# Two short conditionals and one copy of the further steps, in place of two branches that each hold a copy

## The chip, the cores and the metric

The kernel runs on one core of a Trainium2 chip. The metric is the device time of one execution in microseconds. The kernel before took 668.89 us, the median of three runs (668.12 to 669.98). A separate execution was taken by the hardware profiler, and every time inside the kernel below comes from that one: it took 649.77 us in all, of which 648.1 us lie between its first and its last instruction (the span).

The engines go by these names: PE is the matrix engine, PEld its loading of weights, DVE the vector engine, ACT the scalar engine, POOL the GpSimd engine, and SP the engine that here only issues DMA transfers. A "q" behind a name (PEldq, POOLq, SPq) is the sequencer of that engine, which reads instructions, branches, and waits for semaphores.

## What is computed

Attention within chunks of 64 tokens feeds a mixture of eight experts, in which each token goes to one expert only:

```python
batch, n_heads, seq, head_dim = (8, 8, 576, 64)
...
scores = scale * np.matmul(q_c, k_c.transpose(0, 1, 2, 4, 3))
...
attn = attn / (np.sum(attn, axis=-1, keepdims=True) + 1e-09)
out = np.matmul(attn, v_c)
...
N, D, E, F = (4608, 512, 8, 1024)
...
logits = xn @ en.T / tau
expert_idx = np.argmax(logits, axis=1)
...
for e in range(E):
    mask = expert_idx == e
    if not mask.any():
        continue
    h = np.maximum(x[mask] @ w1[e], 0.0)
    out[mask] = gate_w[mask, None] * (h @ w2[e])
```

The number of tokens of an expert is known only when the logits are. With the inputs of the reference the experts get 832, 359, 183, 448, 512, 1023, 576 and 675 tokens.

## The kernel before

**Attention and sorting.** Some 170 us of attention and routing come first. Each token's row is scattered by POOL into a table in device memory, `spots`, where the rows of one expert stand together, in groups of 64.

**Steps.** Then come the experts' steps. A step takes two groups at once: rows 0 to 63 of its block are a group that is counted from the low end of the experts, rows 64 to 127 one from the high end. The data fix how many steps are needed: with the counts above there are 73 groups (13, 6, 3, 7, 8, 16, 9 and 11); the first four steps are always two groups of the first and the last expert, and 65 groups are left. These make 32 pairs and one odd group. On the device the number of pairs is `n_steps` and the odd group is `n_odd`, 0 or 1; `groups` (L890) works them out on DVE, at 168.4 to 170.6 us.

Steps 0 to 35 are always run, by a loop that is unrolled (L1168). Step 36, `LEAST`, is the odd group, if there is one: it has 64 rows only. Steps 37 to 44 are run only if there are so many pairs; `more` (L1224) nests one conditional in the other for them, each on all five engines. With these inputs the odd group is there and none of the steps 37 to 44 is.

**One step.** SP loads its rows (`load_x`) and, where the expert changes, the weights (`load_w2` for the second layer, `load_late` for the first). The loads of weights are issued in every case and move nothing where their condition, read from a table, is 0. DVE turns the rows (`turn_xb`), ACT and DVE make the gate (`gates`), PE multiplies by the first layer (`hidden_plain`, or `hidden_fast` in the loop), ACT and DVE bring the result into shape, and `result` (L427) multiplies by the second layer on PE, scales by the gate on ACT (L447), and has POOL scatter the rows to `out` (L454). For the odd group the two halves of a row stand in the two halves of the block, so `result` has DVE compute the places of half rows first (L452).

**The end, which is what the change touches.** The order of every engine is written out by hand: an instruction stands where the program puts it, and waits on semaphores for others. The instructions of the odd group are laid around the result of step 35 (`before_last`), so that PE has something to do while ACT and DVE turn the odd group's hidden layer. Since that holds in one case only, there are two whole branches: with the odd group (hidden layer of 36, result of 35, result of 36, then `more` with all its eight nested steps), and without (result of 35, then `more` with all its eight nested steps again):

```python
with tc.If(odd_one > 0) as if_odd:
    step_alone(LEAST, before_last)
    more(LEAST + 1)
...
with if_odd.Else():
    ...
    before_last()
    ...
    more(LEAST + 1)
```

A conditional becomes a compare and branch on each engine (line L1228 for those of `more`, L1233 for the odd group). Where a body is not run, the engine jumps to a short block in which it raises its own semaphores by what the body would have added, and goes on from there; SP has nine such instructions, POOL waits for its scatters to have landed and raises its eight DMA semaphores with one instruction, INC_SWDGE_SEM. Line L1269 is the program's end: SP waits for every semaphore, POOL drains, and all five engines meet in two barriers.

Of the kernel before, what the change touches and what calls it, by code (L numbers as in the profile page):

```python
# [1 line left out]

# [16 lines left out]
P = 128  # L19
# [6 lines left out]
def kernel(  # L26
# [11 lines left out]
    nc = tc.nc  # L38
# [76 lines left out]

    n_steps = keep.tile([1, 1], I32, name="n_steps")
    n_odd = keep.tile([1, 1], I32, name="n_odd")
    second = keep.tile([P, 1], FP32, name="second")
    bp = ctx.enter_context(tc.tile_pool(name="blk", bufs=2))

    def whole(w):
# [87 lines left out]
    def gates(j):  # L209
        for _ in gate_parts(j):  # L210
            pass
# [212 lines left out]
        swap_next()  # L424
        turn(1)

    def result(j, ps_y):  # L427
        d = mo.pop(j)
        ps = ps_y.tile([P, D], FP32, tag="y", name="y_ps")
        one_group = j == LEAST  # L430
        w = D // 2 if one_group else D
        for c in range(KF):
            for r in range(P // Q):
                t0, s, d0 = (r % 2, 0, w * (r // 2)) if one_group else (r, r // 2, 0)
                nc.tensor.matmul(  # L435
                    ps[Q * r : Q * r + Q, 0:w],
                    lhsT=d["hT"][:, c, Q * t0 : Q * t0 + Q],
                    rhs=w2_sb[s][buf_of(j)][:, c, d0 : d0 + w],
                    start=(c == 0),
                    stop=(c == KF - 1),  # L440
                )
        if one_group:
            S = late_p.tile([P, 3, KD // 2, 2, Q], FP32, tag="S", name="S", bufs=2)
            y = S.rearrange("p a c b i -> p (a c b i)")
        else:
            y = bp.tile([P, D], FP32, tag="y", name="y", bufs=1)
        nc.scalar.activation(y[:, 0:w], ps[:, 0:w], AF.Copy, scale=gate_of.pop(j))  # L447
        to, at, bound = out, spot[:, j % SPOTS, TOK : TOK + 1].bitcast(I32), N - 1
        if one_group:

            at2 = bp.tile([P, 1], I32, tag="at2", name="at2")
            nc.vector.tensor_scalar(at2, at, 2.0, second, ALU.mult, ALU.add)  # L452
            to, at, bound = out.rearrange("n (s d) -> (n s) d", s=2), at2, 2 * N - 1
        ins = nc.gpsimd.indirect_dma_start(  # L454
            out=to,
            out_offset=bass.IndirectOffsetOnAxis(ap=at, axis=0),
            in_=y[:, 0:w],
            in_offset=None,
            bounds_check=bound,
            oob_is_err=False,  # L460
        )
        tc.declare_no_dep(ins.ins, group="rows", reason="blocks hold different tokens")
        tc.add_to_no_dep_group("rows", ins.ins)
# [8 lines left out]
    with (  # L472
# [417 lines left out]
        def groups():  # L890


            half = 0.5 - 0.5 / G
            n_g = one.tile([P, E], FP32, name="n_g")
            nc.vector.tensor_scalar(
                nb[:, 1 : E + 1], rt_ps[:, 3, 0], 1.0 / G, half, ALU.mult, ALU.add
            )
            nc.vector.tensor_scalar(
                nb[:, 1 : E + 1], nb[:, 1 : E + 1], ROUND, ROUND, ALU.add, ALU.subtract
            )  # L900
            left = one.tile([P, E], FP32, name="left")
            nc.vector.tensor_tensor(left, nb[:, 1 : E + 1], done, ALU.subtract)
            nc.vector.tensor_tensor_scan(n_g, ones, left, 0.0, ALU.mult, ALU.add)
            nc.vector.tensor_scalar(off, n_g[:, E - 1 : E], -1.0, second, ALU.add, ALU.mult)
            nc.vector.tensor_tensor(first, n_g, left, ALU.subtract)
            nc.vector.tensor_scalar(mid, n_g[:, E - 1 : E], 0.5, -0.25, ALU.mult, ALU.add)
            nc.vector.tensor_scalar(mid, mid, ROUND, ROUND, ALU.add, ALU.subtract)
            nc.vector.scalar_tensor_tensor(
                out=odd, in0=mid, scalar=-2.0, in1=n_g[:, E - 1 : E], op0=ALU.mult, op1=ALU.add
            )  # L910
            nc.vector.tensor_tensor(ahead, odd, first_s, ALU.mult)


            nc.vector.tensor_scalar(
                jump[:, 0], nb[:, 0:E], -float(G), float(R), ALU.mult, ALU.add
            )
            nc.vector.scalar_tensor_tensor(
                out=jump[:, 0], in0=done, scalar=float(G), in1=jump[:, 0], op0=ALU.mult, op1=ALU.add
            )
# [233 lines left out]
    with (  # L1153
        tc.tile_pool(name="ps_h", bufs=1, space=PSUM, reuse_waits="tile") as ps_h,
        tc.tile_pool(name="ps_y", bufs=2, space=PSUM, reuse_waits="tile") as ps_y,
    ):
        H_PS = [P, G // Q, KF * Q]

        def hidden_plain(j, w1, behind_it=None):
            for s in range(2 if j != LEAST else 1):  # L1160
                ps = bank(ps_h, H_PS)
                for b in range(G // Q):
                    hidden_part(j, s, b, w1, None, None, ps)
                if behind_it is not None:
                    behind_it(s)

        next(first_gates)
        for j in range(LEAST - 1):  # L1168
            n = j + 2

            def turn_next():
                if n < LEAST:
                    turn_xb(n)
                    if n + XBUF < NJ:
                        load_x(n + XBUF)
                    add_x(n)

            def swap_next():
                if NE <= n < LEAST:
                    take_next(n)  # L1180

            if j == 0:
                next(first_gates)
                add_up(0, None, TS)
                next(first_gates, None)
            elif j == 1:
                turn_next()
                add_up(1, None, TS)
# [17 lines left out]
        def before_last():  # L1206
            result(LEAST - 1, ps_y)
            load_w2(LEAST + 1)

        def step_alone(j, between=None):  # L1210
# [7 lines left out]
            if between is not None:  # L1218
                between()
            result(j, ps_y)  # L1220
            if j + 2 < NJ:
                load_w2(j + 2)

        def more(j):  # L1224
            if j == NJ:
                return

            with tc.If(steps > j - NE - 1):  # L1228
                step_alone(j)
                more(j + 1)  # L1230

        had, had_mo, had_gate = dict(xin), dict(mo), dict(gate_of)
        with tc.If(odd_one > 0) as if_odd:  # L1233
            step_alone(LEAST, before_last)
            more(LEAST + 1)
        for now, then in ((xin, had), (mo, had_mo), (gate_of, had_gate)):
            now.clear()
            now.update(then)
# [35 lines left out]
```

## Time and profile before

| Engine | busy us | share of the span | instructions |
|---|---|---|---|
| PE | 615.0 | 95% | 9744 |
| DVE | 423.6 | 65% | 1124 |
| ACT | 428.6 | 66% | 748 |
| POOL | 188.0 | 29% | 266 |

| What | us |
|---|---|
| median of three runs | 668.89 |
| the profiled execution | 649.77 |
| its span | 648.1 |
| last matrix product ends | 635.8 |
| last scatter to `out` is issued | 636.6 |

Busy time is the time in which an engine worked; waits, branches and the issuing of transfers by a sequencer don't count in it. PE is busy nearly all along, and from 168 us on it has two idle stretches of over 0.25 us only, 1.12 us at 224 us (before a product that waits for a load of weights) and 0.56 us at 443 us. What it has done by 635.8 us is followed by 12.3 us in which it does nothing. Those belong to the lines L454, L1228 and L1269.

### The profile page before, as it was taken

To read this page: it belongs to the slowest core of one execution; us is meant where nothing else is said; L and a number is where in the kernel's file an instruction comes from. 1 tells how busy PE (TensorE), PEld (TensorE's weight loads), DVE (VectorE), ACT (ScalarE), POOL (GpSimd) and SP (SyncE) were. 2 spreads that over 40 slices of the span, in tenths; PEclk is the share of its full clock that TensorE was granted. 3 is DMA by queue.
4 is the path that set the end of the run, shared out by engine and by line. 5 is a ranking of instruction groups with operands and counts; after the bars stand their busy time and mean duration, and the time that the engine had idled before them with its cause. 6 is when DMAs were issued, how large, how long until landed. Compare 5 with 4: busy or idle time off the path is not lost. (4 is left out here: it accounts for less than half of the span.)

```text
span 648.1 us, 24845 instructions
## 1 busy us (share of the span) xinstructions
PE 615.0 (95%) x9744; PEld 350.5 (54%) x9744; DVE 423.6 (65%) x1124; ACT 428.6 (66%) x748; POOL 188.0 (29%) x266
## 2 busy tenths in 40 slices
PE   6999989899899999999999999999999999999992
PEld 5888878776346544554455445664444444444431
DVE  3888888875797645469766647978466576644520
ACT  4767767664218667776777777777776777777640
POOL 7768997752512000120210003212100030001001
PEclk9999999999999999999999999999999999999997
DMA  9999999998488211115785113868711126211110
GB/s 249 309 278 282 276 294 289 347 319 312 157 298 309 66 32 52 45 42 197 265 312 177 41 47 95 320 253 301 269 54 42 45 75 240 76 35 51 35 36 32
DMA packets 91695, 112.67 MB, mean 174 GB/s; under 512 B 49260, under 2 KB 69484, under 8 KB 91560
## 3 DMA queue, kind: packets, MB, share of 16 engines
q1 hardware_dynamic: 77400, 63.60, 30.9%
q0 software_dynamic: 14128, 47.28, 21.0%
q8 instruction: 81, 1.33, 0.8%
q14 instruction: 54, 0.44, 0.2%
q10 hardware_dynamic: 32, 0.02, 0.0%
HBM read 334.71 MB, written 22.69 MB: 551 GB/s over the span
## 5 line engine op out<-in xcount | busy, mean ns | idle before, releaser
L435 PE MATMUL y_ps<-w,hT 128*32 128x512 f32 (+1 forms) x2368 | 277.3, 586 | 1.3 <-DMA w<-in_moe_w_dram 1.3
L383 ACT ACTIVATE h<-C 64x256 f32<-64x256 f32 x264 | 179.2, 679 | 69.9 <-DVE C L396 67.0
L435 PEld LDWEIGHTS y_ps<-w,hT 128*32 128x32 f32 x2368 | 93.7, 110 | 150.6 <-issue 132.0
L454 POOL DMA_INDIRECT out_dram<-y,spot x36 | 38.1, 1060 | 380.1 <-ACT y L447 288.8
L364 PE MATMUL h<-sums,xbT 128*32 128x256 f32 x1056 | 107.0, 379 | 0.6 <-DVEq L321 0.6
L364 PE MATMUL h<-w,S 128*32 128x256 f32 x1056 | 106.7, 379 | 0.0
L396 DVE TENSOR_TENSOR C<-C,h 128x256 f32<-128x256 f32 x231 | 96.1, 416 | 11.2 <-PE h L364 4.4
L390 DVE STREAM_TRANSPOSE hT<-h 128x512 f32<-128x512 f32 x66 | 46.7, 708 | 55.2 <-ACT h L383 54.5
L364 PE MATMUL h<-w,xbT 128*32 128x256 f32 x1056 | 82.0, 379 | 0.0
L364 PEld LDWEIGHTS h<-sums,xbT 128*32 128x32 f32 x1056 | 49.3, 110 | 21.5 <-DVEq L321 1.5
L364 PEld LDWEIGHTS h<-w,xbT 128*32 128x32 f32 x1056 | 44.0, 110 | 31.1 <-issue 8.8
L364 PEld LDWEIGHTS h<-w,S 128*32 128x32 f32 x1056 | 49.5, 110 | 20.6
L225 DVE TENSOR_SCALAR rn<-rn 128x1 f32<-128x1 f32 x33 | 5.0, 152 | 84.3 <-ACT rn L222 84.3
L447 ACT ACTIVATE y<-y_ps,gate 128x512 f32<-128x512 f32 x36 | 24.8, 688 | 48.4 <-issue 43.0
L364 PE MATMUL h<-sums,S 128*32 128x256 f32 x528 | 53.1, 379 | 0.0
L843 POOL DMA_INDIRECT spots<-xr,dest x36 | 37.5, 1040 | 29.1 <-DVE rs L703 10.2
L201 DVE STREAM_TRANSPOSE xbT<-xin 128x256 f32<-128x256 f32 x73 | 44.2, 643 | 0.5 <-DVE hT L390 0.5
L222 ACT ACT_TABLE_LOAD x33 | 42.3, 1283 | 0.9 <-issue 0.4
L229 ACT ACT_TABLE_LOAD x33 | 42.3, 1283 | 0.6
L725 ACT COPY xT<-tr 128x512 f32<-128x512 f32 x36 | 21.1, 586 | 28.9 <-PE tr L723 28.9
L613 POOL DMA_DIRECT2D kx<-in_k_dram x36 | 31.9, 890 | 11.1 <-PE tr L639 10.5
L613 POOL DMA_DIRECT2D qx<-in_q_dram x40 | 34.4, 864 | 0.8 <-PE tr L639 0.7
(218 smaller groups left out, 805.7 us busy)
## 6 DMA issues: line engine op xcount, KB each, us to landing
w<-in_moe_w_dram SPq DMA_DIRECT2D x72, 2048.0 KB
next_w<-in_moe_w_dram SPq DMA_DIRECT2D x65, 2048.0 KB
xin<-spots SPq DMA_DIRECT2D x158, 64.0 KB
qx<-in_q_dram POOLq DMA_DIRECT2D x32, 256.0 KB, 5.2
v<-in_v_dram SPq DMA_DIRECT2D x58, 128.0 KB
kx<-in_k_dram POOLq DMA_DIRECT2D x28, 256.0 KB, 5.4
w<-in_moe_w_dram POOLq DMA_DIRECT2D x2, 2048.0 KB, 13.7
next_w<-in_moe_w_dram POOLq DMA_DIRECT2D x2, 2048.0 KB
```

The costliest lines, as they stand in the source:

```text
L201: nc.vector.transpose(xT[:, :, cols].rearrange("p c (b i) -> p b c i", i=Q), t[:, s * (D // 2) : (s + 1) * (D // 2)].rearrange("p (b i c) ...
L222: nc.scalar.activation(rn, spot[:, j % SPOTS, SQ : SQ + 1], AF.Sqrt)
L229: nc.scalar.activation(sh, sh, AF.Exp, accum_out=gate)
L364: nc.tensor.matmul(ps[t0 : t0 + Q], lhsT=a[:, c, s], rhs=w[:, r], start=c == 0, stop=c == KD // 2 - 1,)
L383: nc.scalar.activation(h[b][G * v : G * v + G, s].rearrange("p (k i) -> p k i", i=Q), x[G * s : G * s + G].rearrange("p (i k) -> p k i", i=Q),
L390: nc.vector.transpose(hT.rearrange("p k (s b i) -> p b s k i", b=2, i=Q)[:, b], h[b].rearrange("p s (k i) -> p s k i", i=Q),)
L396: nc.vector.tensor_tensor(out, a, b, op)
L435: nc.tensor.matmul(ps[Q * r : Q * r + Q, 0:w], lhsT=d["hT"][:, c, Q * t0 : Q * t0 + Q], rhs=w2_sb[s][buf_of(j)][:, c, d0 : d0 + w], start= ...
L447: nc.scalar.activation(y[:, 0:w], ps[:, 0:w], AF.Copy, scale=gate_of.pop(j))
L454: ins = nc.gpsimd.indirect_dma_start(out=to, out_offset=bass.IndirectOffsetOnAxis(ap=at, axis=0), in_=y[:, 0:w], in_offset=None, bounds_ch ...
L613: eng.dma_start(out=x[done : done + n], in_=src[b, :, s : s + n, :].rearrange("h p d -> p h d"),)
L843: ins = nc.gpsimd.indirect_dma_start(out=spots, out_offset=bass.IndirectOffsetOnAxis(ap=at, axis=0), in_=m, in_offset=None, bounds_check=S ...
```

## The change

`result` is cut into `scaled` (products and scaling) and `scatter` (places and transfer). Three things follow.

1. In place of two whole branches there are two short conditionals on the odd group: one around `turn_xb`, `gates` and `hidden_plain` of step 36, one around its products and scaling. Between them, outside of any conditional, stand the load of the rows of step 39, a POOL memset that clears the odd group's output tile, the result of step 35, and the loads of weights for step 37. The load of second-layer weights for step 38, which both branches issued, is moved into the conditional of step 37.
2. `more(LEAST + 1)`, with the eight nested further steps, is written once, behind the second conditional.
3. The odd group's scatter is written behind it and is issued in every case. Where there is no odd group its places are pushed beyond the last row, so that nothing is written. For this `second` (0 for rows 0 to 63, 1 for the rest) becomes one of two columns of a tile `by_half`, and the other column, `half_row`, is `second` plus 9216 where `n_odd` is 0. `groups` gets two instructions on DVE for it.

```diff
-    def result(j, ps_y):
+    def result(j, ps_y, y=None, when=nullcontext):
+        if y is None:
+            y = bp.tile([P, D], FP32, tag="y", name="y", bufs=1)
+        with when():
+            scaled(j, ps_y, y)
+        if j != LEAST:
+            scatter(j, y)
+
+    def scaled(j, ps_y, y):
...
-        nc.scalar.activation(y[:, 0:w], ps[:, 0:w], AF.Copy, scale=gate_of.pop(j))
+        nc.scalar.activation(y, ps[:, 0:w], AF.Copy, scale=gate_of.pop(j))
+
+    def scatter(j, y):
         to, at, bound = out, spot[:, j % SPOTS, TOK : TOK + 1].bitcast(I32), N - 1
-        if one_group:
+        if j == LEAST:
 
             at2 = bp.tile([P, 1], I32, tag="at2", name="at2")
-            nc.vector.tensor_scalar(at2, at, 2.0, second, ALU.mult, ALU.add)
+            nc.vector.tensor_scalar(at2, at, 2.0, half_row, ALU.mult, ALU.add)
...
             nc.vector.tensor_tensor(ahead, odd, first_s, ALU.mult)
+            nc.vector.tensor_scalar(half_row, odd, -2.0 * N, 2.0 * N, ALU.mult, ALU.add)
+            nc.vector.tensor_tensor(half_row, half_row, second, ALU.add)
...
             with tc.If(steps > j - NE - 1):
+                if j == LEAST + 1:
+                    load_w2(j + 1)
                 step_alone(j)
                 more(j + 1)
 
-        had, had_mo, had_gate = dict(xin), dict(mo), dict(gate_of)
-        with tc.If(odd_one > 0) as if_odd:
-            step_alone(LEAST, before_last)
-            more(LEAST + 1)
...
-        with if_odd.Else():
-            del xin[LEAST]
-            load_x(LEAST + XBUF)
-            before_last()
-            load_w2(LEAST + 2)
-            load_late(LEAST + 1)
-            more(LEAST + 1)
+        def when_odd():
+            return tc.If(odd_one > 0)
+
+        with when_odd():
+            turn_xb(LEAST)
+            gates(LEAST)
+            hidden_plain(LEAST, next_w1)
+        load_x(LEAST + XBUF)
+        S = late_p.tile([P, 3, KD // 2, 2, Q], FP32, tag="S", name="S", bufs=2)
+        y_odd = S.rearrange("p a c b i -> p (a c b i)")[:, 0 : D // 2]
+        nc.gpsimd.memset(y_odd, 0.0)
+        result(LEAST - 1, ps_y)
+        load_w2(LEAST + 1)
+        load_late(LEAST + 1)
+        result(LEAST, ps_y, y_odd, when_odd)
+        more(LEAST + 1)
+        scatter(LEAST, y_odd)
```

More of the change, by code (lines that the diff above doesn't have):

```diff
@@ L1 @@
-from contextlib import ExitStack
+from contextlib import ExitStack, nullcontext
 import concourse.bass as bass
@@ L117 @@
     n_odd = keep.tile([1, 1], I32, name="n_odd")
-    second = keep.tile([P, 1], FP32, name="second")
+    by_half = keep.tile([P, 2], FP32, name="by_half")
+    second, half_row = by_half[:, 0:1], by_half[:, 1:2]
     bp = ctx.enter_context(tc.tile_pool(name="blk", bufs=2))
@@ L441, in result @@
                 )
-        if one_group:
[L443 to L447, printed above, removed]
+        nc.scalar.activation(y, ps[:, 0:w], AF.Copy, scale=gate_of.pop(j))
+    def scatter(j, y):
         to, at, bound = out, spot[:, j % SPOTS, TOK : TOK + 1].bitcast(I32), N - 1
-        if one_group:
+        if j == LEAST:
             at2 = bp.tile([P, 1], I32, tag="at2", name="at2")
-            nc.vector.tensor_scalar(at2, at, 2.0, second, ALU.mult, ALU.add)
+            nc.vector.tensor_scalar(at2, at, 2.0, half_row, ALU.mult, ALU.add)
             to, at, bound = out.rearrange("n (s d) -> (n s) d", s=2), at2, 2 * N - 1
@@ L456, in result @@
             out_offset=bass.IndirectOffsetOnAxis(ap=at, axis=0),
-            in_=y[:, 0:w],
+            in_=y,
             in_offset=None,
@@ L1204, with step_alone @@
         odd_one = number(n_odd, 1, ENG.PE, ENG.DVE, ENG.Activation, ENG.Pool, ENG.SP)
[L1206 to L1210, printed above, removed]
+        def step_alone(j):
             turn_xb(j)
@@ L1217, in step_alone @@
                 load_late(j + 1)
-            if between is not None:
-                between()
             result(j, ps_y)
@@ L1228, in more @@
             with tc.If(steps > j - NE - 1):
+                if j == LEAST + 1:
+                    load_w2(j + 1)
                 step_alone(j)
                 more(j + 1)
-        had, had_mo, had_gate = dict(xin), dict(mo), dict(gate_of)
-        with tc.If(odd_one > 0) as if_odd:
-            step_alone(LEAST, before_last)
-            more(LEAST + 1)
-        for now, then in ((xin, had), (mo, had_mo), (gate_of, had_gate)):
-            now.clear()
-            now.update(then)
-        with if_odd.Else():
-            del xin[LEAST]
-            load_x(LEAST + XBUF)
-            before_last()
-            load_w2(LEAST + 2)
-            load_late(LEAST + 1)
-            more(LEAST + 1)
+        def when_odd():
[14 more added lines that the diff above has]
+        scatter(LEAST, y_odd)
 _INS = ['q', 'k', 'v', 'moe_expert_emb', 'moe_tau', 'moe_w1', 'moe_w2']
```

## The prediction

> **What bounds the kernel.** First the page. The span is 648.1 us, the profiled execution 649.77 us, and what fills them is PE; of the chain that ended last PE's two lines make 26% and idle issuing 4%.
>
> ```profile
> PE 615.0 (95%) x9744; PEld 350.5 (54%) x9744; DVE 423.6 (65%) x1124; ACT 428.6 (66%) x748; POOL 188.0 (29%) x266
> ...
> q8 instruction: 81, 1.33, 0.8%
> q14 instruction: 54, 0.44, 0.2%
> ```
>
> The change leaves PE's products alone: in the instruction orders of both kernels, which need no chip, the same products stand in the same sequence. So I look at the end, in the timeline from 634 us on (start, length, engine, line).
>
> ```profile
> 633.43 0.97 POOL L454 DMA_INDIRECT out_dram<-y,spot  x1 [9.35 <-ACT y L447]
> 633.71 2.11 PE L435 MATMUL y_ps<-w,hT 128*32 128x256 f32 x32
> ...
> 634.02 3.77 SPq L172 DMA_DIRECT2D w<-in_moe_w_dram  x4
> 635.87 0.47 ACT L447 ACTIVATE S<-y_ps,gate 128x256 f32<-128x256 f32 x1 [2.72 <-PE y_ps L435]
> 636.62 0.97 POOL L454 DMA_INDIRECT out_dram<-S,at  x1 [2.22 <-ACTq L1228]
> ```
>
> PE is done at 635.82, and the odd group's rows leave at 636.62. Then 11.5 us follow without any engine busy. What fills them stands in the views of lines L1228 (the further steps' conditionals) and L1269 (the end): minimum/median/maximum length in ns, then first and last start.
>
> ```profile
> L1228 SPq EVENT_SEMAPHORE  x9: 17/17/17, 641.7 to 642.3; - x9
> L1228 POOLq EVENT_SEMAPHORE  x4: 17/43/4752, 636.6 to 641.5; - x4
> L1228 PEldq COMPARE_BRANCH  x2: 3574/4304/5034, 634.1 to 637.9; - x2
> L1228 SPq COMPARE_BRANCH  x2: 38/44/50, 637.8 to 642.4; - x2
> L1228 POOLq INC_SWDGE_SEM  x1: 1150/1150/1150, 641.6 to 641.6; - x1
> ```
>
> ```profile
> L1269 SPq EVENT_SEMAPHORE  x14: 17/28/28, 645.5 to 648.1; - x14
> L1269 POOLq DRAIN  x3: 46/103/4084, 643.2 to 647.8; - x3
> ```
>
> POOL's path: scatter at 636.6; 4.75 us until it has landed; 1.15 for INC_SWDGE_SEM; about 0.4 for a branch (642.8 to 643.2); a drain of 4.08, to 647.3; 0.8 for the two barriers. SP's path: its branch over the further steps at 637.8, nothing until 641.7 (3.9 us), nine semaphores, a second branch at 642.4, nothing until 645.5 (3.1 us), ready at about 646.3. POOL is last, by 1.0 us. The change rebuilds both paths.
>
> **The change part by part.**
>
> *Conditionals around the products.* PE meets one more compare that falls through and two jumps over two instructions each. PE's sequencer is ahead of its array: it met L1228 at 634.1, 1.7 us before the last product ended. Short jumps are shown on the other engines only:
>
> ```profile
> L321 POOLq COMPARE_BRANCH  x70: 38/45/55, 199.4 to 598.4; - x70
> L321 DVEq COMPARE_BRANCH  x70: 47/56/72, 203.5 to 606.8; - x70
> ```
>
> From such a branch to the skipped side's semaphore (199.4 to 199.6, 203.5 to 203.7) it is 0.2 us. Hidden below 1.7 us on PE: nothing. PE's own two jumps took 3.6 and 5.0 us. If a short one cost 3.6 like those, 1.9 us would show; none can gain. I take 0, since distance separates the rows. Here a rule of the Trainium skill speaks against the change: "Runtime: NRT & Kernel Launch", section "Instruction fetch mechanics", says that a taken branch whose target lies outside the current window of two pages of 16 KiB (256 instructions each) stalls for a fetch, and advises against runtime control flow. By its warning alone, two more jumps at 3.6 us less the cover would cost up to 3.8 us. By its own measure, a target three instructions ahead lies inside and costs nothing, which the 0.2 us rows bear out. The page sizes don't hold everywhere: by the two queues above, 1.33 MB / 81 is 16 KB per fetch, 0.44 MB / 54 only 8 KB.
>
> *One copy of the further steps.* Before, each engine jumped twice: over the eight steps, then over the whole other branch. In the order of instructions the second jump is 851 on PE, 329 on SP, 137 on DVE, 132 on ACT; it becomes 2 to 4. So SP loses its second wait, 3.1 us, and PE its 5.0 us; of these SP's was on a path 1.0 us from the last. The first jump stays, 286 instructions on SP (277 before).
>
> *SP's loads.* Moved into a conditional that isn't run: the two loads of step 38's weights. SP's four in the row took 3.77 us, 1.23 us apart. Between the rows of step 39 (done at 630.0, plus 0.2 for a short jump) and SP's long branch now stand step 37's two second-layer loads, then its two first-layer loads. The first waits for step 35's result, whose scaling began at 632.5: at 632.4. Three more at 1.23 us: 636.1. Two branches behind it: 636.45, against 637.8. The long jump: 3.9 us and 3.1 us are the rows; I take 3.5, so SP raises its semaphores from 639.95, up to 0.4 us later each (nine took 0.6).
>
> *The new wait.* The half-row places were ready at 627.7 (a DVE instruction of 0.17 us). Now that instruction stands behind the further steps and waits for SP's semaphores of loads, because those steps could reload the table `spot` that it reads. This is SP's long jump put ahead of the scatter. DVE: 640.35 plus 0.1 to wake and 0.17: 640.65. Behind it only the end is queued on DVE; POOL's scatter waits for it.
>
> *POOL.* The memset (128x256; 128x512 took 0.56 us, so some 0.3 as an estimate) falls into the 9.35 us in which POOL waits for ACT: nothing, and 0.3 us if that cover were gone. Scatter of step 35 at 633.4 as before. Then the further steps' skipped side: wait until step 35's rows have landed, at most 4.75 us, 638.2; INC_SWDGE_SEM 1.15, to 639.4; so POOL stands ready 1.3 us before DVE. **Odd scatter at 640.75**, not 636.62: 4.1 us later. But the 4.75 us of landing and the 1.15 us no longer stand between it and the drain. POOL issues (0.97), branches (0.4) and drains: from 642.1. The landing (2.7/3.4/5.5 us for all scatters of this line) runs beside the drain: by 644.15, at 646.25 at worst. SP, waiting for it alone, is ready 0.8 us later, 645.0.
>
> *The drain.* No row says what its 4.08 us are. Ends: nothing of its own beyond the landing, or 4.08 whatever stands before. By the nearest row, the same instruction in the same place, I take 4.08: 646.2. With 0.8 for the barriers the span ends at 647.05.
>
> *Two more instructions on DVE* at 170 us: `ahead` there took 0.16 us, so 0.3 to 0.4 us later for the pad scatters and the first loads of rows. PE has no gap there; its next is 1.12 us at 224 us, on a load. 0 to 0.4; I take 0, PE having been covered throughout.
>
> **Sum.** 648.1 - 647.05 = 1.05 us less, 649.77 to 648.7 in the profiled execution. The runs' median is 668.89, 19.1 us above that execution; the tail doesn't run on PE, so I carry the difference as microseconds: **667.8 us**. That is 0.16%. About 0.3%, 2.0 us, is what a measurement of this kernel tells from no change: the forecast is no difference that shows.
>
> **Rivals.**
>
> *The drain is short* (20%). If the 4.08 us were the remains of what went before (fetches after two long jumps, the landing), SP's 645.0 is the end: 645.05 + 0.8 = 645.85, 2.25 us less: 666.6. For it: the other two drains took 0.10 and 0.05 us. Against: in the trace everything issued by POOL had landed before the drain began.
>
> *The 4.08 us belong to INC_SWDGE_SEM* (14%), the other side. If POOL were busy behind that instruction until its work is over, 1.15 + 0.4 + 4.08 = 5.6 us, the scatter would queue behind it, from 637.8 to 638.2 to some 643.6; landing 4.75 as the last one did: 648.35, SP 0.8 and barriers 0.8: 650.0, 1.9 us more: 670.8. It decides as soon as POOL is held past 642 us. For it: the drain stands right behind INC_SWDGE_SEM. Against: INC_SWDGE_SEM has its own 1.15 us, and the branch ran after it.
>
> *PE's short jumps fetch* (8%): 1.9 us at step 35's result; SP's loads wait for that, so all behind it moves: 1.05 less becomes 0.85 more, 669.7. For it: PE's only two jumps were slow. Against: their distance, 813 and 851 instructions.
>
> *It doesn't do what it says* (3%): the long jump of SP grows, or the layout moves. The tiles keep their addresses in both programs, so I see no place for it but the jump, with 5 us as on PE: 1.5 us on the forecast, 669.3.
>
> **Numbers.** Forecast 55%, with SP's jump and the landing 666.8 to 668.9. Faster by 0.3%: the short drain, and a fringe of the forecast, 26%. Slower: half of the INC case and what I haven't seen, 16%. Within: 58%. Range: down to the short drain with the runs' scatter (they spread 1.9 us), 665.9; up to the INC case, 670.6.
>
> **What would show it.** Scatter of the odd group at 640.3 to 641.5, waiting for DVE; SP with one silence of 3 to 4 us and not two; PEldq with one long branch; a drain of about 4 us beginning at 642. A drain under 2 us is the first rival; a scatter after 642.5 that waited for nothing but POOL, the second; an idle PE at 624 to 632 us, the third. The forecast is wrong if the span is over 649 or under 646 us.

## The result, and the profile after

The changed kernel took 665.12 us (median of 22 runs, 660.25 to 670.74), the kernel before on the same chip 668.15 us (22 runs, 664.12 to 670.41): a ratio of 0.9957, 95% interval 0.9940 to 0.9974. That is 3.0 us less, where 1.05 us less had been forecast, which would not have shown. Two of the changed kernel's runs, 670.62 and 670.74 us, lie more than 1.5% above its fastest and don't count in the ratio. The profiled execution of the changed kernel took 660.25 us, its span is 658.6 us, and PE's last product ends at 647.98.

Busy times of the engines and the two instruction queues, from the page:

```profile
PE 619.9 (94%) x9744; PEld 340.1 (52%) x9744; DVE 425.2 (65%) x1126; ACT 429.0 (65%) x748; POOL 186.7 (28%) x267
...
q8 instruction: 79, 1.29, 0.8%
q14 instruction: 49, 0.40, 0.2%
```

The work is the same, and seven instruction fetches fewer are made (79 + 49 against 81 + 54). The timeline of the end, as start, length, engine, line:

```profile
645.58 0.97 POOL L460 DMA_INDIRECT out_dram<-y,spot  x1 [8.99 <-ACT y L451]
...
648.07 0.47 ACT L451 ACTIVATE S<-y_ps,gate 128x256 f32<-128x256 f32 x1 [2.77 <-PE y_ps L444]
651.68 0.21 DVE L458 TENSOR_SCALAR at<-spot,by_half 128x1 int32<-128x1 int32 x1 [11.94 <-SPq L1230]
652.79 0.97 POOL L460 DMA_INDIRECT out_dram<-S,at  x1 [6.23 <-DVE at L458]
```

The new wait is there: the places are computed at 651.68, released by SP, and the scatter leaves 4.81 us after the last product instead of 0.80. The views of the further steps' conditionals (now L1230) and of the end (now L1276), columns as before:

```profile
L1230 SPq EVENT_SEMAPHORE  x9: 17/17/17, 651.1 to 651.7; - x9
L1230 POOLq EVENT_SEMAPHORE  x4: 17/43/2828, 645.8 to 648.8; - x4
...
L1230 PEldq COMPARE_BRANCH  x1: 4075/4075/4075, 646.5 to 646.5; - x1
...
L1230 SPq COMPARE_BRANCH  x1: 50/50/50, 648.5 to 648.5; - x1
...
L1230 POOLq INC_SWDGE_SEM  x1: 1130/1130/1130, 648.9 to 648.9; - x1
```

```profile
L1276 SPq EVENT_SEMAPHORE  x14: 17/28/3398, 651.8 to 658.5; - x14
...
L1276 POOLq DRAIN  x3: 46/109/5198, 652.6 to 658.3; - x3
```

SP and PE jump once where they jumped twice; SP is silent from 648.5 to 651.1, 2.6 us. The drain's record begins while the scatter is still waiting to go; it ends at 657.76, 4.0 us after the scatter's issue (652.79 + 0.97). SP's wait for the landing ends at 655.20 (651.80 + 3.40), so the drain outlasts it by 2.56 us and sets the end. The stretch from the last product to the end is 10.63 us; it was 12.29.

So the end gives 1.66 us between these two profiles, and their spans do not agree with the runs at all: 648.1 us before, 658.6 after, for a kernel that the runs call faster. The 10 us lie ahead of the experts' steps. The grouping on DVE starts at 168.4 us before and at 179.0 after, with the same instructions up to there. The two profiles are thus of different situations, and the sign of the change cannot be read from them.

### The profile page after: what moved, and what is told of

Read it like the earlier page. It is cut to its first block, busy times and chain, and to the rows that moved or that the text cites. A ratio compares the mean times of both kernels' runs of the same rounds, so it can differ in the third digit from the quotient of the medians.

```text
span 658.6 us, 24851 instructions
## 1 busy us (share of the span) xinstructions
PE 619.9 (94%) x9744; PEld 340.1 (52%) x9744; DVE 425.2 (65%) x1126; ACT 429.0 (65%) x748; POOL 186.7 (28%) x267
## 5 line engine op out<-in xcount | busy, mean ns | idle before, releaser
L444 PE MATMUL y_ps<-w,hT 128*32 128x512 f32 (+1 forms) x2368 | 273.4, 586 | 0.6 <-issue 0.5
L444 PEld LDWEIGHTS y_ps<-w,hT 128*32 128x32 f32 x2368 | 86.8, 110 | 159.2 <-issue 151.4
L397 DVE TENSOR_TENSOR C<-C,h 128x256 f32<-128x256 f32 x231 | 96.1, 416 | 11.2 <-PE h L365 4.4
L365 PE MATMUL h<-sums,xbT 128*32 128x256 f32 x1056 | 96.3, 379 | 0.6 <-DVEq L322 0.6
L365 PE MATMUL h<-w,S 128*32 128x256 f32 x1056 | 95.8, 379 | 0.0
L391 DVE STREAM_TRANSPOSE hT<-h 128x512 f32<-128x512 f32 x66 | 46.7, 708 | 55.0 <-ACT h L384 54.3
L365 PE MATMUL h<-w,xbT 128*32 128x256 f32 x1056 | 76.3, 379 | 0.0
L365 PEld LDWEIGHTS h<-w,xbT 128*32 128x32 f32 x1056 | 42.2, 110 | 31.7 <-issue 9.8
L365 PE MATMUL h<-sums,S 128*32 128x256 f32 x528 | 47.8, 379 | 0.0
L202 DVE STREAM_TRANSPOSE xbT<-xin 128x256 f32<-128x256 f32 x73 | 44.9, 653 | 0.5 <-DVE hT L391 0.5
```

Of the source, the lines that this page charges most:

```text
L202: nc.vector.transpose(xT[:, :, cols].rearrange("p c (b i) -> p b c i", i=Q), t[:, s * (D // 2) : (s + 1) * (D // 2)].rearrange("p (b i c) ...
L365: nc.tensor.matmul(ps[t0 : t0 + Q], lhsT=a[:, c, s], rhs=w[:, r], start=c == 0, stop=c == KD // 2 - 1,)
L391: nc.vector.transpose(hT.rearrange("p k (s b i) -> p b s k i", b=2, i=Q)[:, b], h[b].rearrange("p s (k i) -> p s k i", i=Q),)
L397: nc.vector.tensor_tensor(out, a, b, op)
L444: nc.tensor.matmul(ps[Q * r : Q * r + Q, 0:w], lhsT=d["hT"][:, c, Q * t0 : Q * t0 + Q], rhs=w2_sb[s][buf_of(j)][:, c, d0 : d0 + w], start= ...
```

## The experiments

The runs fell on five chips, named A to E here. Half-clock stretches are described below the first table.

**The same two kernels on other chips.** No edit: e1, e13, e16 and e18 are the changed kernel, e2, e12, e17 and e19 the kernel before.

> The changed kernel once more, for a second profile and a second ratio beside the others of this call. The tail (end of the last matrix product to the end of the span) was 12.3 us before and 10.6 us in the first profile of the changed kernel, 1.7 us less, while the measured times differ by 3.0 us. If the tail is all there is, it comes out at 10.3 to 11.0 us again and the ratio at 0.997 to 0.998. If something ahead of the tail gains as well (theory B), the ratio stays at 0.996 and the time up to the last product is 1 us or more shorter than in the kernel before run in this call.

> The kernel before, unchanged, timed against itself: ratio 1.000 with an interval that shows what this call can tell. Its profile gives a second tail: 12.3 us again if the tail is fixed by its waits, 10.5 to 14 if the landing of the last scatter (4.75 us in the first profile, 3.4 in the median of all) changes from run to run. Attention took until 186.9 us in the first profile of before and until 201.2 us in that of the changed kernel (start of the first scaling of a result); if that is the run and not the kernel, it lies near 200 us here too.

> The kernel before once more, unchanged: no difference, within 0.2%. Its profile gives, beside the changed kernel's on the same chip, the stages: grouping at 170 to 183 us, first step's result, fifth step's result, last product, and the stretch behind it (10.0 or 12.3 us so far).

> The changed kernel once more, unchanged. Theory T (only the stretch behind the last product differs, 10.6 us against 10.0 to 12.3): a ratio between 0.997 and 1.001 on any chip. Theory C (the first stages differ too, by an amount that depends on the chip): about 0.996 where the kernel before takes 668 us, about 1.003 where it takes 651 us, and the profile shows the difference ahead of the fifth step's result.

> The changed kernel, unchanged. Theory G (the sign comes from the granted clock): on a chip where before takes 668 us, the ratio is near 0.996 and the mean clock of the runs of before lies about 0.004 below that of after (1.6 stretches of 3.41 us at half clock); on a chip where before takes 651 us the clocks are alike and the ratio is near 1.003. Theory C (stages): clocks alike, the ratio still below 1 on a chip of 668 us.

> The kernel before, unchanged: within 0.2% of itself. By theory G its profile has more half-clock stretches ahead of 240 us than the changed kernel's on a chip of 668 us, and apart from those the same stage times as the changed kernel's up to the fifth step's result; by theory C the stages differ with no such stretches.

> The kernel before, unchanged: within 0.2% of itself. On a chip where it takes 668 us, theory G (granted clock): mean clock of its runs about 0.988 and two to four half-clock stretches ahead of 240 us in the profile. Theory C (stages): no more stretches than the changed kernel, and stages that differ without them.

> The changed kernel, unchanged. Theory G: on a chip of 668 us ratio near 0.996 with a mean clock 0.004 higher than that of before; on a chip of 651 us ratio 1.001 to 1.003 with the same clock as before. Theory C: on a chip of 668 us a ratio near 0.996 with the same clock as before.

| chip | before, us | changed, us | changed / before | before / itself |
|---|---|---|---|---|
| of the result | 668.15 | 665.12 | 0.9957 [0.9940, 0.9974] | |
| A (e1, e2) | 651.06 | 652.74 | 1.0033 [1.0014, 1.0052] | 0.9994 [0.9968, 1.0019] |
| B (e13, e12) | 651.75 | 653.96 | 1.0028 [1.0005, 1.0051] | 0.9993 [0.9969, 1.0017] |
| C (e16, e17) | 651.9 | 652.75 | 1.0009 [0.9986, 1.0032] | 1.0019 [0.9988, 1.0050] |
| D (e18, e19) | 650.51 | 652.82 | 1.0028 [1.0007, 1.0049] | 1.0008 [0.9986, 1.0029] |

On three of these four chips the changed kernel is slower by 0.3%, on the fourth no difference shows. Chip E, where before takes 668.95 us, is like that of the result; the changed kernel itself was not run there, only edits of it. The first profile of before, 649.77 us, is of the 651 us kind, though the times beside it are of the 668 us kind. It describes another situation than the one in which the change was timed.

Stage times of the profiles, worked out from the traces (us; "half clock" is the time at half clock ahead of 240 us; the stages end where DVE computes `nb`, where ACT scales results 0, 4 and 35, and with PE's last product):

```text
run                 half clock  grouping at  to result 0  to result 4  to result 35  behind last product
before                  0          168.4        18.5         46.9         398.7          12.29
e2  before  (A)         3.41       173.3        18.4         47.0         398.1           9.98
e12 before  (B)         3.41       172.0        18.5         47.3         398.2          10.52
e17 before  (C)         0          172.2        18.5         46.9         398.8          10.17
e19 before  (D)         3.41       170.1        18.5         46.9         398.6          12.44
after                   0          179.0        22.2         44.6         398.8          10.63
e1  changed (A)         3.41       172.0        18.7         46.7         398.7          10.62
e13 changed (B)         6.82       173.4        18.7         49.3         399.0          10.58
e16 changed (C)         6.82       171.2        18.7         49.6         398.9          10.61
e18 changed (D)         6.82       172.6        18.7         47.7         398.4          10.64
```

Three things are to be read. The steps from the fifth on are alike. The end is steady in the changed kernel, 10.58 to 10.64 us, and in the kernel before it is 9.98 to 10.52 us in three profiles and 12.29 and 12.44 in two. The long ones are those in which the last scatter takes long to land, as POOL's longest wait in the view of the further steps shows, first of e17, then of e19:

```profile
L1228 POOLq EVENT_SEMAPHORE  x4: 17/43/2417, 640.3 to 642.9; - x4
```

```profile
L1228 POOLq EVENT_SEMAPHORE  x4: 17/43/4905, 638.1 to 643.2; - x4
```

Of the edits of before below, e10 and e11 wait 2.4 and 2.5 us and e7 4.1. The means of the end are 11.08 us before (10.98 with these three) and 10.62 after: the change gains 0.4 to 0.5 us there on the mean, not the 1.66 of the first pair of profiles. It gains 1.7 to 1.8 where the landing is long and loses 0.1 to 0.6 where it is short.

And in the first 240 us the granted clock falls to one half for 3.41 us at a time, never, once or twice in these profiles. By stretches (stretch, length, then busy time of PE, PEld, DVE, ACT, POOL with counts, granted clock, DMA share, GB/s), e16 ahead of and in its half-clock stretch, and then e17 at the same place:

```profile
227.51:230.92 3.41, 1.36 (x8) 0.30 (x12) 3.17 (x10) 2.02 (x4) 0.00 (x0) 1.00 0.13 36
230.90:234.30 3.40, 3.40 (x20) 0.87 (x16) 0.86 (x3) 2.01 (x3) 0.00 (x0) 0.50 0.03 7
```

```profile
225.47:228.88 3.41, 2.55 (x46) 1.96 (x38) 3.24 (x10) 2.22 (x5) 0.00 (x0) 1.00 0.30 86
228.88:232.29 3.41, 3.02 (x24) 0.82 (x28) 2.82 (x8) 2.48 (x4) 0.00 (x0) 1.00 0.02 5
230.90:234.30 3.40, 3.40 (x40) 1.01 (x34) 1.40 (x3) 2.91 (x5) 0.00 (x0) 1.00 0.03 7
```

PE is busy in both from 230.9 to 234.3 us, with 20 products in one and 40 in the other. What stands ahead is PE's wait for the weights of result 4, in the timelines of e16 and of e17, where the second row has the products behind it:

```profile
229.33 1.05 PE L444 MATMUL y_ps<-w,hT 128*32 128x512 f32 x4 [2.04 <-DMA w<-in_moe_w_dram]
230.61 8.33 PE L444 MATMUL y_ps<-w,hT 128*32 128x512 f32 x58 [0.22 <-DMA w<-in_moe_w_dram]
```

```profile
229.05 1.05 PE L435 MATMUL y_ps<-w,hT 128*32 128x512 f32 x4 [1.04 <-DMA w<-in_moe_w_dram]
230.33 6.63 PE L435 MATMUL y_ps<-w,hT 128*32 128x512 f32 x58 [0.22 <-DMA w<-in_moe_w_dram]
```

The same 58 products take 8.33 us in e16 and 6.63 in e17: a stretch costs up to 1.7 us.

In the ten profiles of the table every half-clock stretch begins within 1.7 us of the end of such a gap of PE, of 1.4 us or more; some gaps of that size have none behind them. What tells most of them apart is how much of one window of time the gap takes. Within a profile the stretches begin a whole number of times 3.413 us apart, the one at the end of the kernel included (in e16 32 times from 121.7 to 230.9 us, and 121 times from there to 643.9). Cut into windows on that grid, from 12 to 250 us, all ten stretches follow a window in which PE was busy for 0.18 to 0.55 of the time; three other windows are as low (0.48, 0.48 and 0.53) without a stretch behind them, and none above 0.55 has one. In e16 the window is busy for 1.36 of 3.41 us, 0.40. In e17 the gap is shorter and falls across two windows, 0.75 and 0.89. The Trainium skill ("TensorE: Matmul & The Clock Gate", "What's actually happening") has the rule: half clock is what PE falls back to when idle, judged by free-running windows of 3413 ns. The 3.41 us and the luck of the phase fit it; its one idle window of about 3.4 us doesn't, as PE was busy for up to 0.55 of that window here.

One such stretch lowers the mean clock of a run by 0.0026 (1.7 / 650). The idle end of the kernel lowers it too, since PE is at half clock there (7.96 us of the span of before, 5.64 of after), so a shorter end raises it without a stretch less. On chip E the eleven runs of before have a mean clock of 0.9875; the changed kernel in the runs of the result has 0.9919, the three edits of it on chip E (e5, e6 and e8 below) 0.991, 0.9907 and 0.9933. If half of what their ends are shorter than 11.08 us is taken off, this is an estimated 0.6 to 1.6 stretches fewer, 1 to 2.7 us, where the gain on record is 3.0. And in the runs of the result time goes with the clock: those of the changed kernel at 0.995 and 0.996 took 660.25 to 664.73 us, those at 0.988 and 0.989 took 666.4 to 668.99. On chips A to D before has 0.9925 to 0.9934 and the changed kernel 0.9921 to 0.9933: alike. Twelve further runs of before on each of chips C and D have 0.9913, which shows how far such a mean can stray. So the clock can carry a good part of the gain on record (theory G of the expectations). It is not shown: the clocks of before in the runs of the result are not known, and no profile of before was had on a chip of 668 us.

A second thing differs there, ahead of result 0. It comes 22.2 to 22.3 us after the grouping in the four profiles on such chips (after, e5, e6 and e8) and 18.7 in the changed kernel on chips A to D. What comes late is ACT's scaling of the first hidden layer behind the grouping, 10.0 to 10.1 us after it in the four and 3.1 us in every profile on chips A to D and in the first of before; first in the timeline of after, then in that of e1:

```profile
189.03 0.66 ACT L286 ACTIVATE h<-h_ps 128x256 f32<-128x256 f32 x2 [10.71 <-remote]
```

```profile
175.08 0.66 ACT L286 ACTIVATE h<-h_ps 128x256 f32<-128x256 f32 x2 [3.78 <-PE h_ps L276]
```

Some 2 us of it come back by result 4, whose weights are then there in time (44.6 to 44.9 us against 46.7 to 49.6). How much before loses here on such a chip is not known; in e7, an edit of it on chip E, that scaling comes after 5.0 us. So this stage can move the 3.0 us either way, and what delays ACT there stays open.

The clock doesn't carry all of the 0.3% on chips A, B and D, but the wait for result 4's weights may carry some: it is 1.12, 1.23, 1.53, 1.04 and 1.10 us in the five profiles of before, with no half-clock stretch behind it, and 0.85, 1.83, 2.04 and 1.86 us in e1, e13, e16 and e18, with one behind it in e13 and e16.

**One part of the change, or its order undone.** e3 is the kernel before without the second branch. It leaves out everything behind the loop where the number of groups is even, which it isn't here. e4 is the changed kernel with the scatter put ahead of the further steps.

```diff
--- before, e3
-        with tc.If(odd_one > 0) as if_odd:
+        with tc.If(odd_one > 0):
             step_alone(LEAST, before_last)
             more(LEAST + 1)
-        with if_odd.Else():
...
--- changed, e4
-        more(LEAST + 1)
         scatter(LEAST, y_odd)
+        more(LEAST + 1)
```

> The kernel before without its branch for no odd group (left out; with these inputs it is never run): the order within the odd branch, its scatter ahead of the further steps and its waits stay, only the second long jump of each engine goes. Forecast's theory: POOL is last and keeps landing, semaphore raise and drain, so the tail loses at most what PE's second fetch added to the landing, 0 to 1.4 us (10.9 to 12.3 us); ratio 0.998 to 1.000. Theory B (less code or fewer long jumps is the gain by itself): ratio 0.995 to 0.997, and the moved scatter has no part in it.

> The changed kernel with the odd group's scatter ahead of the further steps; conditionals, one copy and loads stay as changed. Theory of the moved scatter: the landing and the raising of semaphores stand between scatter and drain again, so the tail is 0.8 + 3.4 (to 4.75) + 1.15 + 0.4 + 4.1 + 0.8 = 10.7 to 12.0 us, 0.1 to 1.4 us more than as changed. Theory of one copy alone: no different from the changed kernel, 10.6 us. A scatter that costs by being late (4.1 us later, behind SP) would make this one the faster of the two by 1 us or more.

On chip A: e3 1.0012 [0.9991, 1.0034], e4 1.0026 [1.0007, 1.0045]. Behind the last product e3 takes 9.64 us and e4 10.00. In both POOL is last, with the scatter at 0.8 and 1.35 us, a landing of 2.4, INC_SWDGE_SEM of 1.15 and a drain of 4.00 us. In the kernel before it is not, where the landing is short. In e12 POOL's drain ends at 648.4 us (644.3 + 4.08), and SP, delayed by its second long jump, has done its waits at 648.9 only:

```profile
L1269 POOLq DRAIN  x3: 46/103/4076, 644.3 to 649.5; - x3
L1269 SPq DRAIN  x3: 7/7/13, 648.9 to 649.2; - x3
```

In e17 SP is 0.2 us behind POOL's drain, in e2 0.05. So with a short landing the second copy costs 0.3 to 0.9 us of the end (9.64 against 9.98, 10.52 and 10.17), of which POOL's own path has 0.3; this is too little to show in the time of e3's runs. And with the scatter ahead the end is 0.6 us shorter than in the changed kernel, as short as that of e2, but the 0.3% remain: they are not made by the end.

**The end taken apart.** e5 computes the places ahead of the further steps. e6 has one drain of POOL more, after the result of step 34, where POOL waits for ACT anyway. e8, and e15 again, have both.

```diff
--- changed, e5
         load_late(LEAST + 1)
+        at2_of[LEAST] = at2 = bp.tile([P, 1], I32, tag="at2", name="at2")
+        odd_at = spot[:, LEAST % SPOTS, TOK : TOK + 1].bitcast(I32)
+        nc.vector.tensor_scalar(at2, odd_at, 2.0, half_row, ALU.mult, ALU.add)
         result(LEAST, ps_y, y_odd, when_odd)
--- changed, e6
             result(j, ps_y)
+            if j == LEAST - 2:
+                nc.gpsimd.drain()
```

> The changed kernel with the half-row places of the odd group computed ahead of the further steps; the scatter itself still stands behind them. Theory 1 (the stretch behind the last product is set by DVE's wait for SP's long jump, then the scatter, then a drain of 4.0 us): the scatter leaves some 2.6 us earlier, at about 2.2 us after the last product instead of 4.8, waiting for POOL itself or ACT, and the stretch from the last product to the end falls from 10.6 to about 8.0 us, then set by POOL's drain or SP's landing wait. Rival (the end is set by landing and the barriers whatever the scatter waits for): 10 us or more. Time of the runs: 2.6 us (0.4%) below the changed kernel on the same chip by theory 1.

> The changed kernel with one drain of POOL more, two steps before the end, where POOL is idle. Theory 1 (the last drain has a fixed length of about 4.0 us, whatever stands before it): the last drain is again 4.0 to 5.2 us, the stretch behind the last product 10.6 us as without it. Rival (the drain works off what all of POOL's earlier transfers of the kernel left): the early drain takes up to 4 us beside PE's work, the last one well under 2 us, and the stretch falls by about 2 us, to where the landing and SP's path end it.

> The changed kernel with both edits, places early and a drain ahead. By theory 1 the same as the places alone: about 8 us behind the last product. If the early drain shortens the last one: bound by the landing of the odd rows, about 7 to 7.5 us behind the last product, so 3 us (0.5%) below the changed kernel.

> The changed kernel with the places early and the drain ahead, once more. If the 7.6 us behind the last product are the kernel's own: about 3 us (0.45%) below the changed kernel on this chip, whatever the chip, so 0.998 of before on a chip of 651 us and 0.991 on one of 668 us.

e5 missed its 8.0 us: 10.32. Its scatter no longer waits for DVE, but POOL itself was late, in its profile with the long landing of step 35's rows:

```profile
L1230 POOLq EVENT_SEMAPHORE  x4: 17/43/4356, 649.5 to 654.1; - x4
...
L1230 POOLq INC_SWDGE_SEM  x1: 1130/1130/1130, 654.1 to 654.1; - x1
```

The scatter went at 4.50 us behind the last product; with the 2.8 us landing of the other profiles it would have gone an estimated 1.5 us earlier. e6 overturned what the forecast took of the drain. First the early drain, in the view of its line in e15, then the end's line there:

```profile
L1204 POOLq DRAIN  x1: 5048/5048/5048, 625.2 to 625.2; - x1
```

```profile
L1281 SPq EVENT_SEMAPHORE  x14: 17/28/1647, 642.0 to 645.2; - x14
...
L1281 POOLq DRAIN  x3: 46/109/3878, 639.9 to 645.0; - x3
```

The early drain takes 5.05 us (5.04 in e6) beside PE's products, in a wait for ACT. After it the last drain ends at 643.75, 0.11 us after SP's wait for the landing (641.99 + 1.65 = 643.64). In e6 the two stand at 658.84 and 658.73, in e8 at 658.09 and 657.99; in the changed kernel at 657.76 and 655.20. And INC_SWDGE_SEM fell from 1.13 to 0.20 us in all three. So the 4.0 us are no fixed price of a drain. Nor are they the price of POOL's first one, since every profile has one at the start of the kernel, which takes 0.18 us, as in after:

```profile
L1267 POOLq DRAIN  x1: 184/184/184, 0.4 to 0.4; - x1
```

They are work that is left by what POOL has done since, which a drain has to do once, and which can be done where POOL is idle. That POOL's transfers leave it is likely, but no run varies their number alone. With it gone the landing sets the end: 8.83 us behind the last product in e6, 7.57 and 7.09 with the places early (e8 and e15).

In the runs: on chip E e5 0.9898 [0.9867, 0.9929], e6 0.9924 [0.9896, 0.9953], e8 0.9908 [0.9876, 0.9940]; on chip C e15 0.9987 [0.9960, 1.0014], where the changed kernel has 1.0009 [0.9986, 1.0032]. Both edits together are thus ahead of before where that takes 668 us and not told apart from it where it takes 651 us; on chip C their median is 2.1 us under the changed kernel's (650.63 against 652.75), in the direction of the 3.0 to 3.5 us of the profiles, though the two intervals overlap.

**The two instructions on DVE.** e9 is the changed kernel without them; it leaves out the case of an even number of groups. e7 and e10 are the kernel before with the pair ten times over. e7 declares a tile of its own for it, e10 uses the tile of the change. e11 has only the tile and one memset.

```diff
--- before, e10
+    by_half = keep.tile([P, 2], FP32, name="by_half")
+    second, half_row = by_half[:, 0:1], by_half[:, 1:2]
...
+            for _ in range(10):
+                nc.vector.tensor_scalar(half_row, odd, -2.0 * N, 2.0 * N, ALU.mult, ALU.add)
+                nc.vector.tensor_tensor(half_row, half_row, second, ALU.add)
--- before, e11 (e7 has this tile as half_row, and the ten pairs)
+    shift = keep.tile([P, 1], FP32, name="shift")
+    nc.vector.memset(shift, 0.0)
```

> The kernel before, with the two instructions that the change added on DVE in the grouping stage written ten times over (20 instructions, result unused). Theory A (they stand on the path to the first rows): the first step's result comes some 20 x 0.16 = 3.2 us later, the time rises by 0.5%, and the change's own pair is worth 0.3 us. Theory B (they lie beside other work): no difference, within 0.2%; then the pair explains nothing of the differences between the two kernels.

> The kernel before with the pair written ten times, as in the ten pairs run, but with the tile laid as the change lays it, so that every other tile keeps its address (there 32 bytes more moved all later tiles). Theory S (the 13 us of the ten pairs run came from the shift of the tiles by 32 bytes): now between 0 and 3.2 us more than before, and nothing lost ahead of the grouping. Theory A (they came from the instructions): again about 13 us more.

> The changed kernel without the two instructions added on DVE in the grouping stage; the half-row places take the flag of the upper half in their place, so the kernel leaves out the case of an even number of groups, which these inputs don't have. If the pair moves the first steps' results (either way): a difference of 0.2% or more to the changed kernel, seen between grouping and fifth result. If it lies beside other work: the same as the changed kernel within 0.1%.

> The kernel before with one more small tile behind the upper-half flag, which moves all later tiles by 32 bytes, and one memset of it. Theory S (the layout makes the loss of the ten pairs run): 10 us or more above before, lost from the first loads on. Rival (that loss was the instructions or the chip): the same as before.

e7 on chip E: 1.0193 [1.0168, 1.0218], 13.6 us more, which fitted no theory of 3 us. e10 on chip B: 1.0041 [1.0020, 1.0062], 2.7 us more; its first result comes 22.2 us after the grouping instead of 18.5. Here ACT's scaling of the hidden layer is in time (3.1 us) and the gates of the first step are late, so this is not the 22.2 us of the chips of 668 us. The pair is thus on the path, at 3.7 / 10 = 0.37 us, and alone it moves the first result by 0.2 (18.7 against 18.5; e9 has 18.5 again). But e9's ratio on chip B, 1.0031 [1.0012, 1.0049], is that of the changed kernel: the pair doesn't make the 0.3%. e11 on chip C: 1.0339 [1.0309, 1.0369], 21.3 us more, from a tile that nothing reads. Its grouping starts at 192.3 us. Its first 30 us by stretches, then those of e17, the kernel before on that chip:

```profile
0.00:30.00 30.00, 15.98 (x213) 13.43 (x214) 9.90 (x23) 10.37 (x16) 14.89 (x30) 0.83 1.03 190
18.30:28.50 10.20, 5.05 (x78) 4.63 (x79) 2.57 (x6) 1.11 (x2) 2.72 (x7) 0.50 1.05 194
```

```profile
0.00:30.00 30.00, 20.44 (x411) 17.31 (x412) 17.06 (x36) 16.48 (x30) 21.62 (x50) 1.00 1.00 271
18.30:28.50 10.20, 8.01 (x197) 6.68 (x195) 7.54 (x16) 7.04 (x15) 7.92 (x23) 1.00 1.03 286
```

The transfers are as busy and move 190 instead of 271 GB/s, and 10.2 us run at half clock. The tile is one of the first, and moves 105 of the 140 named tiles by 32 bytes in on-chip memory. e7 has the same move, e10 has not. The change itself widens the tile `second` from one element to two within its 32 bytes, and no tile moves: the programs' tables of tiles agree on every address. Why the move costs so much stays open.

## Why the prediction was wrong

*The step that failed* is the **sum**: the stretch behind the last product was taken for the whole difference, all that lies ahead of it was put at 0, and the 1.05 us were carried as microseconds from an execution of 649.77 us to runs of 668.89 us. The 19.1 us between them were named and not asked about. By the profiles they arise in the first 250 us, and they vary with the chip. Of the 2.7 us between 667.8 and 665.12, 0.7 are that before itself came out at 668.15, and 2.0 are the change: 3.0 us less in place of 1.05. The end does not make 3.0: it gives 0.4 to 0.5 us on the mean, and 1.8 at most by the ends seen, so that at least 1.2 us lie ahead of the last product, if the end on that chip is one of those seen. What makes this rest stays open. The granted clock can carry 1 to 2.7 us by the mean clocks above, and the stage from the grouping to result 0, which takes the changed kernel 3.5 us longer on such chips, was not seen there for before.

That the changed kernel came out faster, as forecast, is the luck of that chip. On four others it takes 0.9 to 2.3 us more (differences of the medians), with intervals above no change on A, B and D. These 0.3% lie ahead of the last product, since e4 keeps them with another end. Of them the pair's 0.2 us are known. The wait for result 4's weights, 0.4 us longer on the mean and followed by a half-clock stretch in two of four profiles (1.7 us each), would be 1.3 us more. But e9, without the pair, has a wait of 1.41 us and the same 0.3%, and e3, which has neither the pair nor the 0.3%, has one of 2.05 us. So what lengthens it stays open, and the mean clocks of the runs differ by less than half a stretch (0.0013) on each of the four chips.

*Conditionals around the products: cost nothing.* Right. PE's branches of L1239 took 0.09 and 0.19 us. PE's one long jump, of 4.08 us, began 1.5 us before the last product ended and held up no product. The distance and not the number of branches decided, as the rule of the Trainium skill that was weighed there ("Runtime: NRT & Kernel Launch", "Instruction fetch mechanics") measures it.

*One copy: SP's second jump goes.* Right. That POOL was last by 1.0 us holds for the long landing only. Where it is short SP is last, by 0.05 to 0.6 us, and the second copy is worth 0.3 to 0.9 us.

*SP's loads and long jump.* Right in kind; 2.6 us in place of the 3.5 chosen.

*The new wait: the scatter leaves with SP's semaphores, 4.1 us later.* Right in kind: 4.0 us later, waiting for DVE, and DVE for SP. POOL stood ready at 650.0, DVE released it at 651.9. The size is luck: the places were there 3.9 us after the last product and not 4.8, by SP's shorter jump, and the scatter left 0.9 us after them and not 0.1.

*The drain: 4.08 us whatever stands before it.* Right for this change (4.0 us), for the wrong reason. Neither rival on it came: INC_SWDGE_SEM has 1.13 us of its own, and the drain isn't the remains of the last steps either. It works off what POOL's work in the whole kernel has left, and an earlier drain takes that over.

*The end: 11.2 us behind the last product.* 10.63, 0.6 us less, as the drain ends 4.0 us after the scatter's issue and no branch of 0.4 us comes between. But the 12.29 us that it was set against rest on one long landing, 4.75 us; two of five profiles of before have such a one. Against their mean the gain is 0.5 us. The change takes the landing off the path ahead of the drain, and makes the end steady.

*Two instructions at 170 us: taken as 0 of 0 to 0.4.* They move the first result by 0.2 us; in the time of the runs this can't be told (e9).

## What to carry to other kernels

Before a difference in one stage is carried to the time, ask whether the profile and the runs are in the same situation: where they differ by 19 us, eighteen times the expected gain, the sign of the change may be decided elsewhere, and a ratio from one chip is a result for that chip. Where a queue must be drained at the end, drain it once earlier, beside other work, and compute what the last transfer needs ahead of any long jump. A wait that was seen in one profile only (the landing of 4.75 us) is to be looked for in others before it is put into a sum, and so is the engine that comes last: POOL in one, SP in the other.

## What was not expected of the hardware

The granted clock falls in steps of 3.41 us at one half, each worth up to 1.7 us where PE is the bound, none to two in a profile of these two kernels. They stand behind gaps of PE as short as 1.4 us, where these leave PE busy for at most 0.55 of a window of 3.41 us on a fixed grid, so that the phase has a part in it. Moving the tiles by 32 bytes cost 21.3 us of 652, with the transfers' rate in the first 30 us down from 271 to 190 GB/s. The 4 us of POOL's drain at the end could be paid for 15 us earlier, and INC_SWDGE_SEM then took 0.20 us in place of 1.13.
